# The second MoE's first layer as seven block products in two groups of 1024 tokens

## The chip, the cores and the metric

The kernel runs on one core of a Trainium2 chip. A core has TensorE (PE in the profile; its weight loads are PEld), VectorE (DVE), ScalarE (ACT), GpSimd (POOL) and the queue SyncE (SP), which here issues most DMAs; ScalarE's queue issues some. Each engine takes its instructions in order and waits at semaphores for the others. The metric is the device time of one execution in microseconds, the median of several runs.

## The reference

Three steps follow each other. An attention block reads 4 x 512 token rows against 32 state rows each and back, and gives N = 2176 rows (4 x (512 + 32)) of 512 numbers. A first MoE of 8 experts, whose gates are balanced over rows and columns, adds `P[:, e] * (relu(x @ w1[e]) @ w2[e])` over all experts. The second, the part changed here, is one dense layer pair:

```
h = x @ w_in                              # 2176 x 512 times 512 x 2048
g = h * (1.0 / (1.0 + np.exp(-h)))
return (g @ w_out).astype(np.float32)     # times 2048 x 512
```

`w_in` and `w_out` come as float64, everything else as float32.

## The kernel before

Every product of full precision is three matmuls of a high and a low half (fp32r): low x high, high x low, high x high (`mm3`, lines 84 to 86). A matmul has a stationary operand of 128 x 128 and streams up to 512 columns of the other.

The first MoE runs as 16 units (8 experts, two halves of 512 inner columns; line 618), each over 4 batches of 512 tokens and 4 blocks of 128 inner columns: `S1` makes the inner block with 6 matmuls, ScalarE takes its relu into `hh`, VectorE the low half `hl`, and two steps later (`LAG`) `S2` uses both in 12 matmuls of the second layer. The 128 state rows (tile 16) have their own small path (`sr_first`, `sr_turn`). Through units 2 to 15 `convert_some` slips the conversion of the float64 weights between the steps: 32 pieces of 128 x 512, each loaded by SP, nine VectorE operations and a ScalarE cast, then written to DRAM by one DMA from ScalarE's queue as high and low halves side by side (`convert`, line 230).

The second MoE has four slices `v` of 512 inner columns, run over five chunks of tokens (two of 512, three of 384, the state tile being one of them, line 553). Its `S1` streams the turned tokens `x2` (columns) past stationary blocks of `w_in`: 4 blocks of the model dimension x 3 = 12 matmuls for one inner block and chunk. ScalarE makes the sigmoid `sg`, VectorE the product `gv`, ScalarE the high half, VectorE the low half. `turn` (line 600) transposes the first MoE's result on PE, four tiles into one PSUM bank, in unit 15 and the first steps of the second MoE. `load_win` and `load_wout` fetch the converted weights a slice ahead.

PE's order is that of the code; a scheduler places the other engines' instructions. PSUM has eight banks: four for the second layer (`p2`), two for the first (`p1`), two for turns and small sums (`pm`).

## Time and profile before

| what | value |
| --- | --- |
| device time, median of 3 runs | 1671.8 us (1671.42 to 1672.97) |
| span of the profiled execution, first to last instruction (its own time outside the span is not recorded) | 1670.1 us |
| PE / VectorE / ScalarE busy | 1652.0 / 901.1 / 491.4 us |
| mean granted TensorE clock | 0.997 |
| DMA, mean | 133 GB/s |

Busy time counts an instruction from start to end; neighbouring matmuls overlap, so their starts, not their durations, tell what one costs. In the rows, `out<-in` names tiles without buffer numbers, `<-` after the idle time names what the engine waited for.

### The profile page before, as it was taken

The numbers are of one execution on the slowest core, as the hardware profiler recorded it, in microseconds if no ns is written. First come the engines' busy times: TensorE is split into PE (matmuls) and PEld (weight loads), VectorE is DVE, ScalarE is ACT, GpSimd is POOL, SyncE is SP. The second block draws the span as 40 slices with busy tenths as digits, with TensorE's granted clock in tenths as the row PEclk, the third lists the DMA queues.
The fourth block names the chain that finished last, engine by engine and source line by source line (L and its number), as shares of the span: only waits on it lengthen the run. The fifth ranks groups of instructions, "written<-read, shape, count | busy, mean of one in ns | idle before, by whom it ended". The sixth has DMA issues, their size and how long they took to land.

```text
span 1670.1 us, 19780 instructions
## 1 busy us (share of the span) xinstructions
PE 1652.0 (99%) x7660; PEld 1366.2 (82%) x7660; DVE 901.1 (54%) x1541; ACT 491.4 (29%) x887; POOL 15.6 (1%) x25
## 2 busy tenths in 40 slices
PE   7999999999999999999999999999999999999998
...
PEclk9999999999999999999999999999999999999999
...
GB/s 183 14 180 121 85 192 200 170 189 141 194 213 158 205 119 252 133 212 139 199 179 152 214 123 252 128 191 114 161 54 48 4 46 56 9 93 1 89 51 57
DMA packets 107628, 222.03 MB, mean 133 GB/s; under 512 B 28560, under 2 KB 44944, under 8 KB 107536
## 3 DMA queue, kind: packets, MB, share of 16 engines
q1 hardware_dynamic: 101152, 201.76, 41.2%
...
## 4 chain that ended last, share of the span: by engine, by line
PE 85%; DVE 0%; ACT 0%; issue 0%
PE po L84 17%; PE po L86 17%; PE po L85 17%; PE ph L84 10%; PE ph L86 10%; PE ph L85 10%; PE pg L463 3%; PE psr L85 1%; PE psr L86 1%; PE psr L84 1%; PE px L613 0%; PE pt L514 0%; DVE acc L585 0%; DVE l_w L89 0%; DVE accs L585 0%; ACT acc L588 0%
## 5 line engine op out<-in xcount | busy, mean ns | idle before, releaser
L84 PE MATMUL po<-h_w,hl 128*128 128x512 f32 x1024 | 403.1, 394 | 0.0
L86 PE MATMUL po<-h_w,hh 128*128 128x512 f32 x1024 | 398.9, 390 | 0.0
L85 PE MATMUL po<-l_w,hh 128*128 128x512 f32 x1024 | 398.8, 389 | 0.0
L535 DVE SCALAR_TENSOR_TENSOR hl<-ph,hh 128x512 fp32r<-128x512 f32 x256 | 176.6, 690 | 349.3 <-ACT hh L534 348.5
L534 ACT ACTIVATE hh<-ph 128x512 fp32r<-128x512 f32 x256 | 152.9, 597 | 593.6 <-PE ph L86 587.1
L84 PEld LDWEIGHTS po<-h_w,hl 128*128 128x128 f32 x1024 | 192.1, 188 | 50.2 <-issue 11.1
L86 PEld LDWEIGHTS po<-h_w,hh 128*128 128x128 f32 x1024 | 192.2, 188 | 40.6
L85 PEld LDWEIGHTS po<-l_w,hh 128*128 128x128 f32 x1024 | 192.3, 188 | 39.3 <-issue 0.2
L84 PE MATMUL ph<-aTh,G 128*128 128x512 f32 x512 | 203.6, 398 | 1.6 <-DVE hl L535 1.6
L86 PE MATMUL ph<-aTh,G 128*128 128x512 f32 x512 | 199.5, 390 | 0.0
L85 PE MATMUL ph<-aTl,G 128*128 128x512 f32 x512 | 199.5, 390 | 0.0
L589 DVE SCALAR_TENSOR_TENSOR acc<-po,P,acc 128x512 f32<-128x512 f32 x224 | 152.4, 741 | 4.1 <-PE po L86 4.1
L545 DVE TENSOR_TENSOR gv<-ph,sg 128x384 f32<-128x384 f32 (+1 forms) x80 | 48.8, 611 | 191.6 <-ACT sg L543 191.6
L89 DVE TENSOR_TENSOR l_w<-raw_w,h_w 128x512 fp32r<-128x512 f32 x128 | 87.6, 692 | 60.3 <-ACT h_w L203 58.9
L84 PE MATMUL ph<-x2h,wil 128*128 128x384 f32 (+1 forms) x320 | 115.6, 361 | 0.0
L86 PE MATMUL ph<-x2h,wih 128*128 128x384 f32 (+1 forms) x320 | 114.6, 358 | 0.0
L85 PE MATMUL ph<-x2l,wih 128*128 128x384 f32 (+1 forms) x320 | 114.4, 358 | 0.0
L84 PEld LDWEIGHTS ph<-aTh,G 128*128 128x128 f32 x512 | 96.2, 188 | 21.3 <-DVE hl L535 1.9
L86 PEld LDWEIGHTS ph<-aTh,G 128*128 128x128 f32 x512 | 96.1, 188 | 20.4
L85 PEld LDWEIGHTS ph<-aTl,G 128*128 128x128 f32 x512 | 96.2, 188 | 19.2 <-DVE aTl L89 0.2
L543 ACT ACTIVATE sg<-ph 128x384 f32<-128x384 f32 (+1 forms) x80 | 42.7, 534 | 220.5 <-PE ph L86 217.9
L86 PE MATMUL po<-woh,hh 128*128 128x512 f32 x272 | 106.8, 393 | 0.0
...
## 6 DMA issues: line engine op xcount, KB each, us to landing
g_d<-stg SPq DMA_DIRECT2D x120, 512.0 KB, 3.9
G<-g_d SPq DMA_DIRECT2D x240, 256.0 KB, 5.7
raw_w<-in_moe_w_dram SPq DMA_DIRECT2D x136, 256.0 KB, 5.6
raw<-in_moe_w_in_dram SPq DMA_DIRECT2D x16, 512.0 KB, 6.4
wi_d<-cvo ACTq DMA_DIRECT2D x16, 512.0 KB, 2.6
raw<-in_moe_w_out_dram SPq DMA_DIRECT2D x16, 512.0 KB, 6.4
wo_d<-cvo ACTq DMA_DIRECT2D x16, 512.0 KB, 3.2
x<-in_x_dram SPq DMA_DIRECT2D x16, 256.0 KB, 4.1
```

The source lines that it names most:

```text
L84: nc.tensor.matmul(ps, al, bh, start=first, stop=False)
L85: nc.tensor.matmul(ps, ah, bl, start=False, stop=False)
L86: nc.tensor.matmul(ps, ah, bh, start=False, stop=last)
L89: engine.tensor_tensor(out=lo, in0=src, in1=hi.bitcast(F32), op=ALU.subtract)
L463: nc.tensor.matmul(pg[hp, half], a[lanes[half], hp], w[lanes[half]], start=i == 0, stop=i == 2)
L534: nc.scalar.activation(out=hh, in_=ph, func=AF.Relu)
L535: last["dve"] = nc.vector.scalar_tensor_tensor(out=hl, in0=ph, scalar=0.0, in1=hh.bitcast(F32), op0=ALU.max, op1=ALU.subtract)
L543: nc.scalar.activation(out=sg[:, :n], in_=ph[:, :n], func=AF.Sigmoid)
L545: nc.vector.tensor_tensor(out=gv[:, :n], in0=ph[:, :n], in1=sg[:, :n], op=ALU.mult)
L589: nc.vector.scalar_tensor_tensor(out=a, in0=ps, scalar=P[:, t, e:e + 1], in1=a, op0=ALU.mult, op1=ALU.add)
```

## The change

The first layer of the second MoE is computed for two groups of 1024 tokens (eight tiles each). For a slice of 256 inner columns (`phases`: 2 groups x 4 slices `v` x 2 halves `fp` = 16) it is a product of 2 x 2 blocks: two blocks of 128 inner columns, two halves of the model dimension (256 each), two chunks of 512 tokens. Instead of eight block products it takes seven, in Winograd's form of Strassen's scheme: products 1, 2 and 4 take blocks of the weights as they are, the other four sums of them; of the tokens, 1, 2 and 3 take blocks, the others sums. A product is 2 x 3 = 6 matmuls of 512 columns (`product`). Products 1, 6, 7, 4 are added one after another in one PSUM bank, 5 and 3 in another, 2 in a third; ScalarE copies what must be kept between them (`s1`, `s5`, `u2`, `u3`), VectorE adds the parts (`c11`, `c12`, `c22`).

The four sums of weight blocks are made once, in the first MoE, by `convert_in`, which handles two row blocks of `w_in` at a time; its results go to DRAM in pieces of 128 partitions x 2 x 128 (`wi_d`) and as whole rows (`wr_d`). The sums of token blocks are made by `tokens` from float32 copies of the turned tokens (`turn`), for group 0 in unit 15 and for group 1 in phases 6 and 7. Each phase loads the next phase's seven weights behind its own products. Between the products the second layer of the phase before runs in four parts (`second`); the results have tiles of their own (`res`).

The state tile no longer shares a chunk: its turned tokens are stationary and the rows of `w_in` stream past them in 12 matmuls of 512 columns for each `v` (`s_first`, in two halves), its result is turned back (`s_back`) and goes through the second layer in `s_second`.

```diff
+    def convert_in(v, kp):
+
+        both = att.tile([128, 2, FU], F32, tag="att", name=f"wb_{v}_{kp}")
+        for j in range(2):
+            k = kp + 2 * j
+            src = w_in[k * 128:(k + 1) * 128, 2 * v * FU:2 * (v + 1) * FU]
+            tf, af = yield from halves_of(src, f"i{v}_{k}")
+            w = both[:, j]
+            yield V.tensor_tensor(out=w, in0=tf, in1=af, op=ALU.add)
+            hl = att.tile([128, 2, FU], F32R, tag="att", name=f"cvi_{v}_{k}")
+            nc.scalar.copy(hl[:, 0], w)
+            yield V.tensor_tensor(out=hl[:, 1], in0=w, in1=hl[:, 0].bitcast(F32), op=ALU.subtract)
+            nc.scalar.dma_start(out=wr_d[v][k], in_=hl.bitcast(F32))
+            tiles = hl.bitcast(F32).rearrange("p s (f i c) -> p s f i c", f=2, i=2)
+            for i in range(2):
+                if (i, j) != (1, 0):
+                    for s in range(2):
+                        nc.scalar.dma_start(out=wi_d[v][i + j, :, :, s, kp, :].rearrange("f p c -> p f c"), in_=tiles[:, s, :, i])
+        sums = att.tile([128, 4, 2, 128], F32, tag="att", name=f"ws_{v}_{kp}")
+        w4 = both.rearrange("p j (f i c) -> p j i f c", f=2, i=2)
+        a11, a12, a21, a22 = w4[:, 0, 0], w4[:, 1, 0], w4[:, 0, 1], w4[:, 1, 1]
+        yield V.tensor_tensor(out=sums[:, 0], in0=a21, in1=a22, op=ALU.add)
+        yield V.tensor_tensor(out=sums[:, 1], in0=sums[:, 0], in1=a11, op=ALU.subtract)
+        yield V.tensor_tensor(out=sums[:, 2], in0=a11, in1=a21, op=ALU.subtract)
+        yield V.tensor_tensor(out=sums[:, 3], in0=a12, in1=sums[:, 1], op=ALU.subtract)
+        hi, lo = (att.tile([128, 4, 2, 128], F32R, tag="att", name=f"ws{i}_{v}_{kp}") for i in "hl")
+        m = "p m f c -> p (m f c)"
+        nc.scalar.copy(hi.rearrange(m), sums.rearrange(m))
+        yield V.tensor_tensor(out=lo.rearrange(m), in0=sums.rearrange(m), in1=hi.bitcast(F32).rearrange(m), op=ALU.subtract)
+        for s, t in enumerate((hi, lo)):
+            for i in range(4):
+                nc.scalar.dma_start(out=wi_d[v][3 + i, :, :, s, kp, :].rearrange("f p c -> p f c"), in_=t.bitcast(F32)[:, i])
+
...
+    def load_win(v, fp, p):
+        tag = "w1h" if loaded[0] % 2 == 0 else "w1l"
+        loaded[0] += 1
+        w = wp.tile([128, 2, 2, 128], F32R, tag=tag, name=f"wi_{v}_{fp}_{p}_{loaded[0]}", bufs=4)
+        nc.sync.dma_start(out=w.bitcast(F32), in_=wi_d[v][WEIGHT_OF[p], fp])
+        went[p] = w
+
...
         hT[u, b, f] = (hh, hl)
 
...
+    def turn(g, c, k):
+
+        j, kp = divmod(k, 2)
+        if kp == 0:
+            F2[g, j, c] = stp.tile([128, 2, 512], F32, tag="stg", name=f"x2f_{g}_{j}_{c}")
+        pt = pm(f"px2_{g}_{c}_{k}")
+        for i, t in enumerate(chunks[2 * g + c]):
+            nc.tensor.transpose(pt[:, i * 128:(i + 1) * 128], acc_of(t)[:, k * 128:(k + 1) * 128], ident)
+        nc.scalar.copy(F2[g, j, c][:, kp], pt)
+
+    def tokens(g, p, pool=s8, tag="s8"):
+
+        flat = "p k c -> p (k c)"
+        made = {5: ((0, 1), (0, 0)), 6: ((1, 1), 5), 7: ((1, 1), (0, 1)), 4: ((1, 0), 6)}
+        if p in made:
+            src = F2[g, p] = att.tile([128, 2, 512], F32, tag="att", name=f"x2t_{g}_{p}")
+            one, other = (F2[(g, *at) if isinstance(at, tuple) else (g, at)] for at in made[p])
+            nc.vector.tensor_tensor(out=src.rearrange(flat), in0=one.rearrange(flat), in1=other.rearrange(flat), op=ALU.subtract)
...
+            src = F2[g, *{1: (0, 0), 2: (1, 0), 3: (1, 1)}[p]]
+        x = x2[g, p] = pool.tile([128, 2, 2, 512], F32R, tag=tag, name=f"x2_{g}_{p}")
+        nc.scalar.copy(x[:, 0].rearrange(flat), src.rearrange(flat))
+        lo_of(x[:, 1].rearrange(flat), src.rearrange(flat), x[:, 0].rearrange(flat))
+
+    def product(q, p):
+
+        g, v, fp = phases[q]
+        where = {1: "a", 6: "a", 7: "a", 4: "a", 2: "b", 5: "c", 3: "c"}[p]
+        if p in (1, 2, 5):
+            banks[where] = p1(f"pa{q}") if where == "a" else pm(f"p{where}{q}")
+        ps, w, x = banks[where], went[p], x2[g, p]
+        for kp in range(2):
+            ops = ((w[:, 1, kp], x[:, 0, kp]), (w[:, 0, kp], x[:, 1, kp]), (w[:, 0, kp], x[:, 0, kp]))
+            for i, (a, b) in enumerate(ops):
+                begin = p in (1, 2, 5) and kp == 0 and i == 0
+                nc.tensor.matmul(ps, a, b, start=begin, stop=kp == 1 and i == 2, skip_group_check=True)
+
+        if p == 1:
+            kept("s1", "e2", att)
+        elif p == 5:
+            kept("s5", "att", att)
+        elif p == 2:
+            silu(q, 0, 0, summed("c11", ps, parts["s1"]))
+        elif p == 6:
+            kept("u2", "e2", att)
+        elif p == 3:
+            silu(q, 0, 1, summed("c12", ps, parts["u2"]))
+        elif p == 7:
+            kept("u3", "att", att)
+            silu(q, 1, 1, summed("c22", parts["u3"], parts["s5"]))
+        else:
+            silu(q, 1, 0, ps)
+
+    def silu(q, f, c, src):
+        sg = att.tile([128, 512], F32, tag="e2", name=f"sg{q}_{f}_{c}", bufs=3)
+        nc.scalar.activation(out=sg, in_=src, func=AF.Sigmoid)
+        nc.vector.tensor_tensor(out=sg, in0=src, in1=sg, op=ALU.mult)
+        hh = hp_.tile([128, 512], F32R, tag="hh", name=f"gh{q}_{f}_{c}")
+        hl = hp_.tile([128, 512], F32R, tag="hl", name=f"gl{q}_{f}_{c}")
+        nc.scalar.copy(hh, sg)
+        lo_of(hl, sg, hh)
+        blocks[q, f, c] = hh, hl
+
...
+        if f == 0:
+            res_p[q, c] = [bank(f"pr{q}_{t}") for t in tiles]
+        hh, hl = blocks.pop((q, f, c))
+        wh, wl = w2t[g, v, 2 * fp + f]
+        for i, ps in enumerate(res_p[q, c]):
+            s = slice(i * 128, (i + 1) * 128)
+            mm3(ps, hh[:, s], hl[:, s], wh, wl, f == 0, f == 1)
...
+    def s_load(v, half):
+        t = wr[v, half] = s8.tile([128, 2, 2, FU], F32R, tag="s8", name=f"wr_{v}_{half}")
+        nc.sync.dma_start(out=t.bitcast(F32), in_=wr_d[v][2 * half:2 * half + 2].rearrange("k p s f -> p k s f"))
+
+    def s_first(v, half):
+        if half == 0:
+            sp[v] = pm(f"psf{v}")
+        w = wr.pop((v, half))
+        for i in range(2):
+            k = 2 * half + i
+            mm3(sp[v], sx["h"][:, k], sx["l"][:, k], w[:, i, 0], w[:, i, 1], k == 0, k == KD - 1)
+        if half == 1:
+            ps = sp.pop(v)
+            t = sg_of[v] = att.tile([128, FU], F32, tag="e2", name=f"sgs{v}", bufs=3)
+            nc.scalar.activation(out=t, in_=ps, func=AF.Sigmoid)
+            nc.vector.tensor_tensor(out=t, in0=ps, in1=t, op=ALU.mult)
...
-    convert_ops = (op for i in range(NV * (KD + NF)) for op in convert(i))
-    pace = 10 * NV * (KD + NF) / ((NU - 2.5) * B * NF)
+    convert_ops = convert_all()
+    pace = 1.12 * NV * (2 * 23 + NF * 9) / ((NU - 2.5) * B * NF)
     done = [0]
...
+            if u == NU - 1 and 8 <= k < 12:
+                for n in range(2):
+                    turn(0, k % 2, (k - 8) // 2 * 2 + n)
+            if u == NU - 1 and k == 12:
+                s_load(0, 0)
+            if u == NU - 1 and k in (8, 9, 10, 11, 12, 13):
+                for p in {8: (1,), 9: (5,), 10: (2,), 11: (6, 3), 12: (7,), 13: (4,)}[k]:
+                    tokens(0, p)
+
+    ending = [lambda: S2(*steps[-2]), lambda: None, lambda: S2(*steps[-1]), lambda: None]
+    for q, (g, v, fp) in enumerate(phases):
+        more = q + 1 < len(phases)
+        earlier = ending if q == 0 else [lambda n=n: second(q - 1, n) for n in range(4)]
+
+        def step(p):
+            product(q, p)
+            if more:
+                load_win(*phases[q + 1][1:], p)
+            if q == 7 and p != 4:
+                later = {1: 6, 5: 3, 2: 7, 6: 4}.get(p)
+                if later:
+                    tokens(1, later)
+
+        s0 = g == 0 and fp == 0
+        step(1)
+        step(5)
+        step(2)
+        earlier[0]()
+        if q == 0:
+            load_wout(0, 0, 2)
+            s_turn()
+        elif g == 0 and fp == 1:
+            s_back(v)
+        step(6)
+        earlier[1]()
+        if s0:
+            s_first(v, 0)
+            s_load(v, 1)
+        step(3)
+        step(7)
+        earlier[2]()
+        if s0:
+            s_first(v, 1)
             if v + 1 < NV:
-                if b == 3 and f < 2:
-                    load_win(v + 1, f)
-                if b == 4:
-                    if f < 2:
-                        load_win(v + 1, f + 2)
-                    load_wout(v + 1, f)
+                s_load(v + 1, 0)
+        if 3 <= q < 7:
+            turn(1, (q + 1) % 2, (q - 3) // 2 * 2)
+            turn(1, (q + 1) % 2, (q - 3) // 2 * 2 + 1)
+        step(4)
+        earlier[3]()
+        if q == 0:
+            load_wout(0, 0, 3)
+        if g == 0 and fp == 1:
+            s_second(v, 0)
+        elif q and q <= 8 and fp == 0:
+            s_second(phases[q - 1][1], 1)
+        if more:
+            for f in range(2):
+                g1, v1, fp1 = phases[q + 1]
+                if q:
+                    load_wout(g1, v1, 2 * fp1 + f)
+        if q == 6:
+            for p, (pool, tag) in zip((1, 5, 2), ((s8, "s8"), (accp, "acc"), (accp, "acc"))):
+                tokens(1, p, pool, tag)
+    q = len(phases) - 1
+    spare = iter((p1, p1, pm, pm))
+    for n in range(4):
+        second(q, n, p2 if n < 2 else lambda nm: next(spare)(nm))
```

Three places show how the instructions stand. First ScalarE's queue in the first MoE's unit 2, around the conversion: before, one cast `cvo` and one DMA for each piece (`L260`, `wi_d0`), between relus `hh` and weight casts `h_w`; the brackets name the semaphores waited for, `DMAHW` those of earlier DMAs.

```order
L257 CAST cvo_1_2524<-cv_1_2365 128x512 [waits DVE_49]
L534 ACTIVATE hh2_2_1_2534<-ph2_2_1_2527 128x512 [waits PE_49,Activation_49]
L203 CAST h_w1_4_0_2576<-raw_w1_4_0_2574 128x512 [waits DMAHW4_49]
L260 DMA wi_d0_174<-cvo_1_2524 128x1024 [waits DMAHW0_49,DVE_49,Activation_49]
L534 ACTIVATE hh2_2_2_2587<-ph2_2_2_2580 128x512 [waits PE_49]
L203 CAST h_w1_4_1_2615<-raw_w1_4_1_2613 128x512 [waits DMAHW6_49]
L534 ACTIVATE hh2_2_3_2631<-ph2_2_3_2624 128x512 [waits PE_49]
L517 CAST hsh_3_2652<-pt_3_2647 128x512 [waits PE_49]
L534 ACTIVATE hh2_3_0_2675<-ph2_3_0_2668 128x512 [waits PE_49]
```

And now, same place, where the sums of the first pair of row blocks (`wsh`, `wsl`) are written:

```order
L287 CAST wsh_0_0_2624<-ws_0_0_2540 128x1024 [waits DVE_49]
L291 DMA wi_d0_178<-wsh_0_0_2624 128x2x128 [waits Activation_49]
L291 DMA wi_d0_178<-wsh_0_0_2624 128x2x128 [waits DMAHW1_49]
L291 DMA wi_d0_178<-wsh_0_0_2624 128x2x128 [waits DMAHW2_49]
L577 ACTIVATE hh2_2_3_2646<-ph2_2_3_2639 128x512 [waits PE_49]
L291 DMA wi_d0_178<-wsh_0_0_2624 128x2x128 [waits DMAHW3_49]
L291 DMA wi_d0_178<-wsl_0_0_2625 128x2x128 [waits DMAHW5_49,DVE_49]
L291 DMA wi_d0_178<-wsl_0_0_2625 128x2x128 [waits DMAHW6_49]
L291 DMA wi_d0_178<-wsl_0_0_2625 128x2x128 [waits DMAHW7_49]
L291 DMA wi_d0_178<-wsl_0_0_2625 128x2x128 [waits DMAHW0_49]
L561 CAST hsh_3_2667<-pt_3_2662 128x512 [waits PE_49]
L577 ACTIVATE hh2_3_0_2702<-ph2_3_0_2695 128x512 [waits PE_49]
```

One DMA has become eight in a row (others of three and five stand ahead), seven of which wait for the semaphore of an earlier DMA; the relu `hh2_3_0` and the turned state rows `hsh` stand behind them.

Second PE where a group of four tiles is turned (`px2`). Before, early in the second MoE:

```order
L85 MATMUL po16_0_3_10714<-wol_0_1_10577,hh16_0_1_10654 128x512
L86 MATMUL po16_0_3_10714<-woh_0_1_10575,hh16_0_1_10654 128x512
L613 MATMUL px2_3_1_10768<-ident_98,acc2_1250 128x128 [waits DVE_49]
L613 MATMUL px2_3_1_10768<-ident_98,acc3_1450 128x128 x2
L84 MATMUL ph16_1_0_10774<-x2h_1_10471,wil_0_0_10162 128x512 [waits DVE_49]
L85 MATMUL ph16_1_0_10774<-x2l_1_10472,wih_0_0_10160 128x512
L86 MATMUL ph16_1_0_10774<-x2h_1_10471,wih_0_0_10160 128x512
L84 MATMUL ph16_1_0_10774<-x2h_1_10471,wil_0_0_10162 128x512
L85 MATMUL ph16_1_0_10774<-x2l_1_10472,wih_0_0_10160 128x512
```

Now, in phase 6, after the second half of the state tile's first layer (`psf3`, weights `wr_3_1`):

```order
L84 MATMUL psf3_12065<-wr_3_1_12072,sxl_10865 128x512 [waits DMAHW0_49]
L85 MATMUL psf3_12065<-wr_3_1_12072,sxh_10864 128x512
L86 MATMUL psf3_12065<-wr_3_1_12072,sxh_10864 128x512
L84 MATMUL psf3_12065<-wr_3_1_12072,sxl_10865 128x512
L85 MATMUL psf3_12065<-wr_3_1_12072,sxh_10864 128x512
L86 MATMUL psf3_12065<-wr_3_1_12072,sxh_10864 128x512
L629 MATMUL px2_1_1_2_12136<-ident_98,acc2_1254 128x128 [waits DVE_49]
L629 MATMUL px2_1_1_2_12136<-ident_98,acc2_1254 128x128
L629 MATMUL px2_1_1_2_12136<-ident_98,acc3_1454 128x128 x2
L629 MATMUL px2_1_1_3_12142<-ident_98,acc2_1254 128x128 [waits Activation_49]
L629 MATMUL px2_1_1_3_12142<-ident_98,acc2_1254 128x128
L629 MATMUL px2_1_1_3_12142<-ident_98,acc3_1454 128x128 x2
```

Two groups are turned one behind the other, the second waits for ScalarE's copy of the first, and the phase's product 4 and a part of the second layer come behind both; the state's second half waits for its own load.

Third VectorE. Before, at the start of slice 2:

```order
L545 TENSOR_TENSOR gv17_4_3_12030<-ph17_4_3_12015,sg17_4_3_12028 128x384 [waits Activation_49]
L89 TENSOR_TENSOR hl17_4_3_12033<-gv17_4_3_12030,hh17_4_3_12032 128x384 [waits Activation_49]
L545 TENSOR_TENSOR gv18_0_0_12068<-ph18_0_0_12053,sg18_0_0_12066 128x512 [waits Activation_49]
L89 TENSOR_TENSOR hl18_0_0_12071<-gv18_0_0_12068,hh18_0_0_12070 128x512 [waits PE_49,Activation_49]
L545 TENSOR_TENSOR gv18_0_1_12102<-ph18_0_1_12087,sg18_0_1_12100 128x512 [waits Activation_49]
L585 TENSOR_TENSOR accs_1468<-po17_4_16_11995,accs_1468 128x512 [waits PE_49]
L585 TENSOR_TENSOR acc3_1450<-po17_4_14_11996,acc3_1450 128x512 [waits PE_49]
```

Now, where phase 7 begins (`ress` is the state tile's result, `c11_7` the phase's first sum, `gls3` the state's low half):

```order
L775 TENSOR_TENSOR ress_11152<-prs2_1_12179,ress_11152 128x512 [waits PE_49]
L89 TENSOR_TENSOR x2_1_5_12200<-x2t_1_5_12198,x2_1_5_12200 128x1024
L89 TENSOR_TENSOR x2_1_2_12203<-x2f_1_1_0_11923,x2_1_2_12203 128x1024
L89 TENSOR_TENSOR x2_1_6_12219<-x2t_1_6_12217,x2_1_6_12219 128x1024 [waits PE_49,Activation_49]
L89 TENSOR_TENSOR x2_1_3_12233<-x2f_1_1_1_12135,x2_1_3_12233 128x1024 [waits PE_49,Activation_49]
L667 TENSOR_TENSOR c11_7_12243<-pb7_12236,s1_7_12213 128x512 [waits PE_49]
L639 TENSOR_TENSOR x2t_1_7_12254<-x2f_1_1_1_12135,x2f_1_0_1_11720 128x1024
L689 TENSOR_TENSOR sg7_0_0_12245<-c11_7_12243,sg7_0_0_12245 128x512 [waits Activation_49]
L89 TENSOR_TENSOR gls3_12281<-pst3_12275,ghs3_12280 128x512 [waits Activation_49]
L89 TENSOR_TENSOR x2_1_7_12256<-x2t_1_7_12254,x2_1_7_12256 128x1024 [waits Activation_49]
L89 TENSOR_TENSOR gl7_0_0_12249<-sg7_0_0_12245,gh7_0_0_12248 128x512 [waits Activation_49]
```

Operations of 1024 columns for group 1's tokens (`x2_1_...`) stand in the row ahead of the phase's own work.

## Rows read from the trace of the kernel before

**Rows 1.** The page: span, busy time, PE and granted clock in 40 slices.

```profile
span 1670.1 us, 19780 instructions
## 1 busy us (share of the span) xinstructions
PE 1652.0 (99%) x7660; PEld 1366.2 (82%) x7660; DVE 901.1 (54%) x1541; ACT 491.4 (29%) x887; POOL 15.6 (1%) x25
...
PE   7999999999999999999999999999999999999998
...
PEclk9999999999999999999999999999999999999999
```

**Rows 2.** The page, chain of waits: shares by engine.

```profile
PE 85%; DVE 0%; ACT 0%; issue 0%
```

**Rows 3.** Stretches: their us, busy time of each engine, clock, DMA share, GB/s.

```profile
700.00:1100.00 400.00, 400.00 (x1811) 327.19 (x1810) 241.66 (x392) 111.74 (x195) 0.00 (x0) 1.00 0.60 183
...
1400.00:1500.00 100.00, 100.00 (x473) 86.75 (x472) 36.43 (x60) 23.04 (x42) 0.00 (x0) 1.00 0.13 43
```

**Rows 4.** PE's timeline, end of the second MoE: start us, duration, instruction.

```profile
1657.11 0.33 PE L84 MATMUL ph<-x2h,wil 128*128 128x384 f32 x1
...
1659.22 0.39 PE L84 MATMUL po<-woh,hl 128*128 128x512 f32 x1
...
1661.07 0.39 PE L86 MATMUL po<-woh,hh 128*128 128x512 f32 x1
...
1665.15 0.39 PE L86 MATMUL po<-woh,hh 128*128 128x512 f32 x1
```

**Rows 5.** PE's timeline around a turned group in unit 15.

```profile
1245.22 0.60 PE L613 MATMUL px<-ident,acc 128*128 128x128 f32 x4
1245.57 0.49 PE L84 MATMUL ph<-aTh,G 128*128 128x512 f32 x1
...
1249.80 0.39 PE L84 MATMUL po<-h_w,hsl 128*128 128x512 f32 x1
```

**Rows 6.** The page, costliest groups: busy us, mean ns of one, idle before.

```profile
L535 DVE SCALAR_TENSOR_TENSOR hl<-ph,hh 128x512 fp32r<-128x512 f32 x256 | 176.6, 690 | 349.3 <-ACT hh L534 348.5
L534 ACT ACTIVATE hh<-ph 128x512 fp32r<-128x512 f32 x256 | 152.9, 597 | 593.6 <-PE ph L86 587.1
...
L89 DVE TENSOR_TENSOR l_w<-raw_w,h_w 128x512 fp32r<-128x512 f32 x128 | 87.6, 692 | 60.3 <-ACT h_w L203 58.9
```

**Rows 7.** ScalarE's timeline: the copy of that group.

```profile
1245.86 0.59 ACT L614 CAST x2h<-px 128x512 fp32r<-128x512 f32 x1 [2.56 <-PE px L613]
```

**Rows 8.** Lines 152 and 89 by shape: duration ns min/median/max, first and last start.

```profile
L152 ACT CAST bdh<-bd x1: 1047/1047/1047, 11.9 to 11.9; 128x1024 fp32r<-128x1024 f32 x1
...
L89 DVE TENSOR_TENSOR bdl<-bd,bdh x1: 1226/1226/1226, 13.0 to 13.0; 128x1024 fp32r<-128x1024 f32 x1
```

**Rows 9.** DMA: queues (packets, MB, share of 16 engines); issues, median us to landing.

```profile
q1 hardware_dynamic: 101152, 201.76, 41.2%
...
wi_d<-cvo ACTq DMA_DIRECT2D x16, 512.0 KB, 2.6
...
wih<-wi_d SPq DMA_DIRECT2D x16, 256.0 KB, 3.2
```

**Rows 10.** Line 260 on ScalarE's queue: ns of its waits and issues.

```profile
L260 ACTq EVENT_SEMAPHORE  x32: 17/1932/4564, 243.3 to 1130.9; - x32
L260 ACTq DMA_DIRECT2D wi_d<-cvo x16: 326/326/337, 247.1 to 1017.1; - x16
```

**Rows 11.** Waits in 300 to 1240: us in total, times, longest.

```profile
ACT hh L534 <- PE ph L86: 503.1, 197, 6.2
```

More of the change, by code (lines that the diff above doesn't have):

```diff
@@ new lines, in convert_all @@
+    def convert_all():
+        for v in range(NV):
+            for kp in range(2):
+                yield from convert_in(v, kp)
+            for f in range(NF):
+                yield from convert_out(v, f)
+    PRODUCTS = (1, 5, 2, 6, 3, 7, 4)
+    WEIGHT_OF = {1: 0, 2: 1, 3: 6, 4: 2, 5: 3, 6: 4, 7: 5}
+    went = {}
+    loaded = [0]
+    def load_win(v, fp, p):
[4 more added lines that the diff above has]
+        went[p] = w
@@ new lines, in S1 @@
+        gh, gl = G[u, b][:, :, 0], G[u, b][:, :, 1]
+        ah, al = (t[:, b % 2] for t in aT[b // 2])
+        fs = slice(f * 128, (f + 1) * 128)
+        for q in range(2):
+            mm3(ph, gh[:, q, fs], gl[:, q, fs], ah[:, q], al[:, q], q == 0, q == 1)
+        hh = hp_.tile([128, 512], F32R, tag="hh", name=f"hh{u}_{b}_{f}")
+        hl = hp_.tile([128, 512], F32R, tag="hl", name=f"hl{u}_{b}_{f}")
+        nc.scalar.activation(out=hh, in_=ph, func=AF.Relu)
+        last["dve"] = nc.vector.scalar_tensor_tensor(out=hl, in0=ph, scalar=0.0, in1=hh.bitcast(F32), op0=ALU.max, op1=ALU.subtract)
@@ L618, in fused_kernel @@
-    steps = [(u, b, f) for u in range(NU + NV) for b in range(B if u < NU else len(chunks)) for f in range(NF)]
+    F2, x2 = {}, {}
+    def turn(g, c, k):
[6 more added lines that the diff above has]
+        nc.scalar.copy(F2[g, j, c][:, kp], pt)
@@ new lines, in fused_kernel, with kept, summed @@
+    banks, parts, blocks = {}, {}, {}
+    def product(q, p):
[4 more added lines that the diff above has]
+        ps, w, x = banks[where], went[p], x2[g, p]
+        for kp in range(2):
+            ops = ((w[:, 1, kp], x[:, 0, kp]), (w[:, 0, kp], x[:, 1, kp]), (w[:, 0, kp], x[:, 0, kp]))
+            for i, (a, b) in enumerate(ops):
+                begin = p in (1, 2, 5) and kp == 0 and i == 0
+                nc.tensor.matmul(ps, a, b, start=begin, stop=kp == 1 and i == 2, skip_group_check=True)
+        def kept(nm, tag, pool):
+            t = parts[nm] = pool.tile([128, 512], F32, tag=tag, name=f"{nm}_{q}", **({"bufs": 3} if tag == "e2" else {}))
+            nc.scalar.copy(t, ps)
+        def summed(nm, one, other):
+            t = rawp.tile([128, 512], F32, tag="raw", name=f"{nm}_{q}")
+            nc.vector.tensor_tensor(out=t, in0=one, in1=other, op=ALU.add)
+            return t
+        if p == 1:
[13 more added lines that the diff above has]
+            silu(q, 1, 0, ps)
@@ new lines, in second @@
+    def second(q, n, bank=p2):
+        g, v, fp = phases[q]
+        c, f = divmod(n, 2)
+        first, final = (v, fp) == (0, 0), (v, fp) == (NV - 1, 1)
+        tiles = chunks[2 * g + c]
+        if f == 0:
[5 more added lines that the diff above has]
+            mm3(ps, hh[:, s], hl[:, s], wh, wl, f == 0, f == 1)
+        if f == 0:
+            return
+        if first:
+            res[g, c] = accp.tile([128, 4, DM], F32, tag="acc", name=f"res{g}_{c}")
+        for i, (t, ps) in enumerate(zip(tiles, res_p.pop((q, c)))):
+            a = res[g, c][:, i]
+            if first:
+                nc.vector.tensor_copy(a, ps)
+            else:
+                nc.vector.tensor_tensor(out=a, in0=ps, in1=a, op=ALU.add)
+            if final:
+                b, r = divmod(t, R)
+                (nc.sync if t % 2 else nc.scalar).dma_start(out=out[b * ROWS:b * ROWS + S].rearrange("(p r) d -> p r d", r=R)[:, r], in_=a)
```

151 lines of the change are left out of this document (58 added, 93 removed).

## Prediction

> **What bounds the kernel now.** I read the page first. TensorE (PE) is busy 99% of the span and its granted clock stands at 9 tenths or more in every slice, the upper of its two levels, 2.4 GHz; VectorE is busy 54%, ScalarE 29% [rows 1]. The chain of waits puts 85% of the span on PE and next to nothing on any other engine [rows 2]. The table by stretches says the same for the two places the change touches: in the first MoE (700 to 1100) PE has no gap, VectorE is busy 60%, ScalarE 28%, and the DMA engines 0.60; in the second (1400 to 1500) PE again has none, VectorE is at 36%, ScalarE at 23%, DMA at 0.13 [rows 3]. So the end is the sum of PE's instructions, and the price of one is the step from a matmul's start to the next one's, not the duration in its row (0.39), which overlaps with its neighbours. Eighteen second-layer matmuls of 512 columns start from 1661.07 to 1665.15: 4.08/18 = 0.2267 us each. Twelve first-layer matmuls of 384 columns take from 1657.11 to 1659.22: 2.11/12 = 0.1758 each [rows 4].
>
> The sum is made against the profiled execution, whose span is 1670.1; the median of the runs is 1671.8, so 1.7 lie around the span or between executions, and I carry them over unchanged.
>
> **First layer, on PE.** Before, each of 16 column blocks takes 12 matmuls for each of five token chunks: 384 of 512 columns and 576 of 384 columns, 384 x 0.2267 + 576 x 0.1758 = 87.1 + 101.3 = 188.3 us. Now: 16 phases x 7 products x 6 matmuls = 672, and 4 x 12 = 48 for the state tile, all of 512 columns: 720 x 0.2267 = 163.2. Difference -25.1. The second layer stays at 816 matmuls of 512 columns. The products have another order and another pair of operands, but the same shape, so I take the same step for them.
>
> The Trainium skill speaks against the full size of this term: "TensorE: Matmul & The Clock Gate", section "Back-to-back issue gap", puts the isolated warm step at N/2.4 + 2.5 ns, thus 216 and 162.5 ns, by which the estimate would be 720 x 0.2158 - 384 x 0.2158 - 576 x 0.1625 = -21.1. The trace does not agree: the steps are 227 and 176 ns [rows 4], and the sum goes by these.
>
> **Transposes.** 84 in 21 groups of four instead of 68 in 20 groups. One group of four: from 1245.22 to 1249.80 lie the group and 18 matmuls; 4.58 - 18 x 0.2267 = 0.50 us [rows 5]. Sixteen more transposes are +2.0 (between +0.5 for one more group and +2.0).
>
> **What waits in the steady phases.** One phase is 90 matmuls, 20.4 us of PE. ScalarE has 12 operations (4 copies, 4 sigmoids, 4 casts) at 0.60, VectorE 19 (3 sums, 4 products with the sigmoid, 4 low halves, 8 result adds) at 0.69 [rows 6]: 7.2 us (35%) and 13.1 us (64%). Products 1, 6, 7, 4 go one after another into one bank, so each waits until ScalarE has copied what stood there. Closest is product 4 behind the copy u3: between product 7 and it lies one part of the second layer, 12 x 0.2267 = 2.72 us. The sum c12 and one sigmoid stand before the copy on ScalarE, and end about 0.3 after product 7; the copy takes 0.60: about 0.9 to 1.1 of 2.72. The other hand-offs have 0.5 to 1.8 us left. I take 0; if the cover is gone it costs what rival C says.
>
> **The turn into group 1.** In phases 4 and 6 the state tile's sums hold one of the two banks for transposes, so the second group of four waits for ScalarE's copy of the first. In the trace the transposes start at 1245.22, and their copy begins at 1245.86 and takes 0.59 [rows 5, 7]: ready at 1246.45, where the second group would have started at 1245.72. That is 0.75, and 1.0 with part of the state's sigmoid ahead on ScalarE: 2 x 1.0 = +2.0 (0 to 4). Phases 6 and 7 also carry the casts of group 1: VectorE has 42 operations at 0.69 and 11 of 1024 wide at 1.23 [rows 6, 8], 42.5 us, where PE has 204 matmuls and 3 groups of transposes, 47.7 us. At 89% in order, behind four low halves of 1.23 in a row, something comes late: the state's transposed tile waits behind c11_7, the state's second-layer bank behind the result adds. By hand four such places give 0.4 + 0.9 + 0.5 + 0.8 = +2.6 (0 to 6). The turn into the first phase, during unit 15, has seven casts of 1.05 on ScalarE and as many low halves on VectorE [rows 8]; everything is ready but the state tile's low half: +0.2 (0 to 2).
>
> **The state weights' second half.** It may be loaded only when the first half has been read, and is wanted three steps later: 1.36 + 1.36 + 2.72 = 5.44 us. A 256 KB piece lands in 3.2 us. SP's queue moved 201.76 MB in 41.2% of the span: 293 GB/s. So 1 MB costs 3.2 - 0.89 + 3.58 = 5.9 [rows 9]; 0.45 x 4 = +1.8. Bounds: 0, and +12 if it shares the engines with the seven weights (3.0 each). All other loads are issued nearly a phase ahead of their use.
>
> **The conversion, in the first MoE.** VectorE gets 40 more operations, about 21 us over some 900 where it is 60% busy [rows 3]: hidden. ScalarE gets 8 casts of 1024 (1.05 [rows 8]) and issues 144 DMAs in place of 32, in 8 bursts each of three, five and eight. Issuing one takes 0.326, and ahead of each of the 32 the queue stood 1.93 us in the median (0.02 to 4.56) at a semaphore [rows 10]; part of that is VectorE's low half, part the DMA that used the same semaphore before, here often one of SP's. All of this stands ahead of the relus, which the next units need. Before each relu ScalarE now idles 503.1/197 = 2.6 us [rows 11]; a relu may come 5.3 us late (two banks: the next use of a bank is 30 matmuls, 6.8 us, after it was filled, less 0.60 + 0.69 and hand-offs). The short bursts fit (five: 1.6 + 1.9). A burst of eight: 2.6 of issue, 1.9 of wait, and one landing of 2.6 [rows 9] are 7.1; but the scheduler puts relus between its DMAs. I take 0.5 for each of eight bursts: +4 (0 to 36, below).
>
> The Trainium skill, "DMA: Bandwidth & Descriptors", section "Issuing engines are not separate DMA queues", calls the time to initiate a DMA usually small beside the DMA itself. Here it is 0.33 beside 2.6 [rows 9, 10], which agrees; by that rule alone this term would be 0 and the sum -16.5, but the rule counts no waits ahead of the issue, and the row has them.
>
> **Sum.** -25.1 + 2.0 + 2.0 + 2.6 + 0.2 + 1.8 + 4 = -12.5: a span of 1657.6, and 1659.3 for the median. The tail (last add, last output) is the same kind of work. Own range by half and double the waits: 1653 to 1668.
>
> **Rivals.**
> B, all added waits are hidden: -25.1 + 2.0 = -23.1, 1648.7. For it: no engine but PE is above 64% in a steady phase, and before, the PE row shows no waiting at all [rows 3]. Against it: only one bank is free for the turns, which no faster engine mends.
> C, a hand-off in every phase: product 4 waits for u3, or the second layer for a low half. If each of 16 phases loses 0.8, that is +12.8 on top of the sum: 1672.1, no change. For it: seven products have four strict hand-offs where before two banks took turns. Against it: the row order on ScalarE puts u3 ahead of the cast that waits for VectorE, which leaves the slack above.
> D, slower: the first MoE pays, because ScalarE stands at the semaphores of its own 512-byte-piece DMAs and of SP's loads, and relus and copies of the gate products behind it come late. Without the +4 the sum is -16.5; it turns when 24 bursts lose over 0.69 us each. At 1.5 each, 36 us: 1671.8 - 16.5 + 36 = 1691. For it: the wait of 1.93 before a single DMA [rows 10], and that SP's G loads in turn wait for ScalarE's DMAs. Against it: 2.6 us of idle time before each relu [rows 11], and 32 such waits that left PE without a gap.
> E, the change doesn't do what it says: products with a slower step than 0.2267 (other reading pattern, or the clock lower in the gaps). At the 384-column price per column (0.1758/384 x 512 = 0.2344) the 672 cost 5.2 more: 1664.5. It stays on the forecast's side.
>
> **How the numbers follow.** Forecast 0.45 (with E), B 0.23, C 0.17, D 0.12, unnamed 0.03. The predicted time is the forecast's, 1659. A measurement of this kernel tells 0.2%, 3.3 us, from no change. Faster: 0.45 + 0.23 + 0.10 of C + 0.02 = 0.80; same: 0.06 of C and a little of D, 0.08; slower 0.12. The range leaves out the far side of B and D: 1646 to 1675.
>
> **What would show it.** The second MoE, from its first first-layer matmul to PE's last one, 15 to 20 us shorter, with PE gaps of about 1 us at the second turns of phases 4 and 6, at the state's second halves, and at the start of phases 7 and 8, and none in phases 9 to 15. In the first MoE, intervals between units longer by 0 to 1 us. If units grow by 2 us or more, D is right and the forecast wrong; if PE waits before product 4 in every phase, C; if the product step is not 0.2267, the first term falls.

## Result and profile after

The changed kernel takes 1648.5 us in the median (1647.6 to 1649.1) beside 1672.3 for the kernel before in the same rounds: a ratio of 0.9857, 95% interval 0.9843 to 0.987. That is 23.8 us faster; forecast were 12.5, and the number lies within the stated range, 1646 to 1675, nearly on rival B (all added waits hidden, 1648.7).

The page of the changed kernel, first its span, busy times, clock row, DMA queues and the shares of the chain, which answer to [rows 1, 2, 9]:

```profile
span 1645.7 us, 19928 instructions
## 1 busy us (share of the span) xinstructions
PE 1627.0 (99%) x7436; PEld 1328.8 (81%) x7436; DVE 1004.9 (61%) x1676; ACT 543.2 (33%) x946; POOL 15.6 (1%) x25
...
PEclk9999999999999999999999999999999999999999
...
q1 hardware_dynamic: 107168, 239.52, 48.5%
q10 hardware_dynamic: 36848, 33.71, 6.2%
...
PE 94%; DVE 3%; ACT 1%; DMA 1%; issue 1%; SPq 0%; DVEq 0%; ACTq 0%
```

The same stretches as [rows 3] (us, then busy PE, PEld, DVE, ACT, POOL, clock, DMA share, GB/s):

```profile
1400.00:1500.00 100.00, 99.21 (x448) 81.65 (x448) 69.54 (x100) 40.01 (x64) 0.00 (x0) 1.00 0.47 154
...
700.00:1100.00 400.00, 399.33 (x1807) 326.35 (x1807) 249.02 (x411) 115.05 (x200) 0.00 (x0) 1.00 0.65 198
```

PE is as full as before, though VectorE has nearly doubled (36 to 70) in the second MoE, and ScalarE's queue (`q10`) has six times the packets. PE's waits in the changed kernel (us in total, times, longest), the two largest behind the kernel's start:

```profile
PE px L629 <- ACT x2f L630: 1.6, 2, 0.8
PE po L84 <- DVE acc L617: 1.3, 3, 0.7
```

The first row is the forecast wait of the second turned group, 0.8 in place of 1.0 at each of two places. None stands before a product, a part of the second MoE's second layer, or the state's transposes. The second row lies in the first MoE, three places that the kernel before does not have; it is taken up under the conversion below.

Where the time went can be read with one marker: `hs`, the state rows' relu, runs once in each unit, its last in unit 15, ahead of the turns. First before, then after (first and last start):

```profile
L507 ACT ACTIVATE hs<-psr x16: 598/599/600, 138.8 to 1176.9; 128x512 f32<-128x512 f32 x16
```

```profile
L551 ACT ACTIVATE hs<-psr x16: 588/598/600, 136.7 to 1175.7; 128x512 f32<-128x512 f32 x16
```

From the first to the last `hs` the first MoE took 1038.1 us before and 1039.0 after, so the conversion costs 0.9 in this pair of profiles; nine profiles of kernels with this same first MoE go from 1039.0 to 1040.6. From the last `hs` to the span's end it was 1670.1 - 1176.9 = 493.2, and now 1645.7 - 1175.7 = 470.0: the second MoE gained 23.2. The 2.1 before the first `hs` lie at the start, which the change doesn't touch; the first `hs` stands at 136.7 to 138.9 in the profiles of this kernel and of the runs below. This split is used for all of them ("second part" below; the changed kernel has 470.0 and, run again, 469.9).

### The profile page after: what moved, and what is told of

Read it like the earlier page. It is cut to its first block, busy times and chain, and to the rows that moved or that the text cites. A ratio compares the mean times of both kernels' runs of the same rounds, so it can differ in the third digit from the quotient of the medians.

```text
span 1645.7 us, 19928 instructions
## 1 busy us (share of the span) xinstructions
PE 1627.0 (99%) x7436; PEld 1328.8 (81%) x7436; DVE 1004.9 (61%) x1676; ACT 543.2 (33%) x946; POOL 15.6 (1%) x25
## 4 chain that ended last, share of the span: by engine, by line
PE 94%; DVE 3%; ACT 1%; DMA 1%; issue 1%; SPq 0%; DVEq 0%; ACTq 0%
PE po L84 15%; PE po L86 14%; PE po L85 14%; PE ph L84 7%; PE ph L86 7%; PE ph L85 7%; PE pa L659 5%; PE pr L85 4%; PE pr L86 4%; PE pr L84 4%; PE pg L507 3%; PE pc L659 3%; PE pb L659 1%; PE psr L418 1%; PE psr L84 1%; PE psr L86 1%
## 5 line engine op out<-in xcount | busy, mean ns | idle before, releaser
L84 PEld LDWEIGHTS ph<-aTh,G 128*128 128x128 f32 x512 | 96.2, 188 | 21.6 <-DVE hl L578 2.1
L203 ACT CAST h_w<-raw_w 128x512 fp32r<-128x512 f32 x136 | 81.8, 621 | 94.1 <-PE po L86 46.4
L84 PE MATMUL pr<-woh,gl 128*128 128x512 f32 x256 | 99.6, 389 | 0.0
L86 PE MATMUL pr<-woh,gh 128*128 128x512 f32 x256 | 99.6, 389 | 0.0
L85 PE MATMUL pr<-wol,gh 128*128 128x512 f32 x256 | 99.6, 389 | 0.0
L659 PE MATMUL pa<-x,wi 128*128 128x512 f32 x384 | 98.3, 392 | 0.0
L89 DVE TENSOR_TENSOR stg<-pg,stg 128x512 fp32r<-128x512 f32 x120 | 75.7, 684 | 27.1 <-ACT stg L512 27.0
```

The source lines that it names most:

```text
L84: nc.tensor.matmul(ps, al, bh, start=first, stop=False)
L85: nc.tensor.matmul(ps, ah, bl, start=False, stop=False)
L86: nc.tensor.matmul(ps, ah, bh, start=False, stop=last)
L89: engine.tensor_tensor(out=lo, in0=src, in1=hi.bitcast(F32), op=ALU.subtract)
L203: nc.scalar.copy(hi, raw)
L659: nc.tensor.matmul(ps, a, b, start=begin, stop=kp == 1 and i == 2, skip_group_check=True)
```

## Experiments

**Eight products in place of seven.** No sums of weights or tokens; every block of C gets its two products in a bank of its own.

```diff
-        where = {1: "a", 6: "a", 7: "a", 4: "a", 2: "b", 5: "c", 3: "c"}[p]
...
+        f, c, j = p
+        if j == 0:
+            banks[f, c] = (p1 if f == c else pm)(f"p{f}{c}_{q}")
+        ps, w, x = banks[f, c], went[2 * f + j], x2[g, 2 * j + c]
...
-        step(3)
-        step(7)
+        step((1, 1, 1))
+        step((1, 0, 0))
```

> The changed kernel with its groups, phases, state path and order, but each phase multiplies the 2 x 2 blocks out in eight block products in place of seven, without sums of weights or tokens. Theory A (the end is the sum of PE's steps, everything else is hidden): 16 phases x 6 matmuls x 0.2267 = 21.8 us more than the changed kernel, a span of about 1667.5 and a median near 1670, 2 us below the kernel before. Theory B (the products' copies and hand-offs cost something that the trace of waits does not show): less than 21.8 more, since these are gone too; 5 us less would be about 1665.

Measured: 1675.3 us, ratio to before 1.0019 (1.0009 to 1.0028): 26.8 more than the changed kernel, more than either theory said. Of B's sign, less than 21.8, nothing is seen, but waits that came new could hide it. The trace names most of the rest: PE waits before turned groups, which here find both banks for turns taken.

```profile
PE px L614 <- DVE sgs L706: 2.9, 2, 1.5
PE px L614 <- ACT x2f L615: 2.9, 4, 0.8
```

**Eight products, the turned groups where banks are free.**

```diff
-        if 3 <= q < 7:
-            turn(1, (q + 1) % 2, (q - 3) // 2 * 2)
-            turn(1, (q + 1) % 2, (q - 3) // 2 * 2 + 1)
         step((1, 0, 1))
+        if 3 <= q < 7:
+            turn(1, (q + 1) % 2, (q - 3) // 2 * 2)
         earlier[3]()
+        if 3 <= q < 7:
+            turn(1, (q + 1) % 2, (q - 3) // 2 * 2 + 1)
```

> Eight block products as before (kernel eight, 26.8 us above the changed kernel, with 5.8 us of waits of PE before turned groups where the changed kernel has 1.6), but the turned groups of phases 3 to 6 stand behind product 8 and behind the second layer's last part, where banks are free. Theory A: without those waits only the 16 x 6 x 0.2267 = 21.8 us of the eighth product are left, and the 1.6 of the changed kernel's own two waits go too: 20 to 22 above the changed kernel, 1668.5 to 1670.5. If 26 remain, the eighth product costs more than its matmuls.

Measured: 1667.3 us, 0.9972 (0.9959 to 0.9984), 18.8 above the changed kernel, 1.2 below the range expected, and 19.7 to 20.4 above the changed kernel with its own turns apart (next). No wait of PE is listed in the second part any more. It is 1666.0 - 1175.5 = 490.5, against 1644.9 - 1176.2 = 468.7 there: 21.8, theory A's number. The `hs` rows, of this kernel and of the next one (its second profile):

```profile
L536 ACT ACTIVATE hs<-psr x16: 598/598/600, 137.8 to 1175.5; 128x512 f32<-128x512 f32 x16
```

```profile
L551 ACT ACTIVATE hs<-psr x16: 591/598/600, 136.8 to 1176.2; 128x512 f32<-128x512 f32 x16
```

The first MoE gives the difference, 1037.7 without the sums against 1039.0 to 1040.6. So in the second MoE leaving out the eighth product is worth its matmuls, no more and no less, and the sums of weights take 1 to 3 us of that back in the first.

**The turned groups on both sides of product 4**, twice, the second time beside the changed kernel itself.

```diff
             turn(1, (q + 1) % 2, (q - 3) // 2 * 2)
-            turn(1, (q + 1) % 2, (q - 3) // 2 * 2 + 1)
         step(4)
+        if 3 <= q < 7:
+            turn(1, (q + 1) % 2, (q - 3) // 2 * 2 + 1)
```

> The changed kernel, but in phases 3 to 6 the second group of four transposes comes behind product 4 instead of behind the first group. The two waits of 0.8 for ScalarE's copy in the trace of after should go, 1.6 us less than the changed kernel: a span of about 1644 and a median near 1647. If the wait is only moved (product 4 then holds something that the turned group waits for), no change.

> The changed kernel itself, on the same chip and beside the same runs as the next kernel: 1648.5 again, the measure for it.

> The changed kernel with the two turned groups of phases 3 to 6 on both sides of product 4, as before. If the two waits of 0.8 us are really gained, 1.6 less than the changed kernel beside it; if the 1.6 of the first comparison was chance, within 0.5 of it.

Measured: 1646.95 (0.9853, 0.9838 to 0.9868) and 1647.6 (0.9849, 0.9836 to 0.9862); the changed kernel again 1648.6 (0.9859, 0.9846 to 0.9873). The intervals overlap, so the medians alone don't settle it. The trace does: the wait of PE before turned groups has gone, and the second part is 468.7 in both profiles against 470.0 and 469.9. A gain of 1.2 us, not quite the 1.6 that were expected (a wait of 0.2 before a `pr` bank is new); its medians are the lowest of all the kernels here.

**The copy u3 made three and five times over.**

```diff
-            kept("u3", "att", att)
+            u3 = parts["u3"] = att.tile([128, 512], F32, tag="att", name=f"u3_{q}")
+            for _ in range(5):
+                nc.scalar.copy(u3, ps)
```

> The changed kernel, but ScalarE makes the copy u3 five times over, so product 4 is released 2.4 us later in each phase (the cast ahead of the last copies adds up to 0.6). By the slack that the prediction gave (0.9 to 1.1 of 2.72 us used) PE waits 0.8 to 1.4 in each of 16 phases: 13 to 22 us more than the changed kernel, 1662 to 1670, rival C made real. If the cover is larger than read, no change (1648.5).

> The changed kernel, but the copy u3 made three times over: product 4 is released 1.2 us later in each phase. With five copies (2.4 us and up to one cast more) the loss was 16.9 us, 1.06 in each phase, so 1.3 to 1.9 of the cover is free: three copies stay inside it, no change (within 2 us of the changed kernel). If ScalarE's row as a whole is what costs, half of the 16.9: 8 us more.

Measured: five copies 1665.4 (0.9961, 0.9946 to 0.9976), 16.9 more; three 1649.95 (0.9868, 0.9853 to 0.9882), 1.4 more. With five, PE waits where rival C said:

```profile
PE pa L659 <- ACT u L683: 7.6, 10, 0.8
PE px L629 <- ACT x2f L630: 3.6, 2, 2.2
```

The listed 7.6 is less than the loss: the second part is 15.2 longer, 1.0 a phase in the mean. With three no wait before product 4 is listed; the second part is 1.5 longer, 0.6 of it before turned groups (2.2 in place of 1.6). 1.2 us are covered, 2.4 are not: some 1.4 are free, near the 1.6 to 1.8 that the prediction read from the order of ScalarE's queue, and C needs more than that to come true.

**The weight pieces in twice as many DMAs.**

```diff
-                        nc.scalar.dma_start(out=wi_d[v][i + j, :, :, s, kp, :].rearrange("f p c -> p f c"), in_=tiles[:, s, :, i])
+                        for h in range(2):
+                            nc.scalar.dma_start(out=wi_d[v][i + j, h, :, s, kp, :], in_=tiles[:, s, h, i])
...
-                nc.scalar.dma_start(out=wi_d[v][3 + i, :, :, s, kp, :].rearrange("f p c -> p f c"), in_=t.bitcast(F32)[:, i])
+                for h in range(2):
+                    nc.scalar.dma_start(out=wi_d[v][3 + i, h, :, s, kp, :], in_=t.bitcast(F32)[:, i, h])
```

> The changed kernel, but every 128 KB piece of the converted weights goes out as two DMAs of 64 KB: 224 in place of 112 on ScalarE's queue, bursts of 16 in place of 8. Slack theory: ScalarE pays 112 x 0.48 = 54 us more of issue, but PE sees only what passes 5.3 us in front of a relu: a burst of 16 takes 7.7 of issue, so 0 to 2.4 in each of 8: 0 to 19 us more, most likely under 5. Rival D as it was meant (ScalarE's queue is near its limit): 20 to 50 us more.

Measured: 1653.2 (0.9892, 0.9877 to 0.9907), 4.7 more. The first MoE takes 1043.6 in place of 1039.0; the second part is unchanged (469.8). The loss has one kind of place, where the gate products `pg` need a bank that a late `hl` still holds:

```profile
PE pg L509 <- DVE hl L580: 4.7, 4, 1.4
```

One of the four, 0.4, is in the changed kernel too; the other three, 1.43 to 1.44 each, are new. They do not stand behind bursts of 16, after which no wait of PE is listed, but behind bursts of nine, which are five in the changed kernel. ScalarE's, VectorE's and PE's rows at the first of them: six DMAs, the last of the nine, end where the relu `hh` starts.

```profile
560.94 3.19 ACTq L278 DMA_DIRECT2D wi_d<-cvi  x6
564.17 0.60 ACT L579 ACTIVATE hh<-ph 128x512 fp32r<-128x512 f32 x1 [4.75 <-DMA wi_d<-cvi]
565.55 0.50 PE L509 MATMUL pg<-h_w,stl 64*128 64x512 f32 x1 [1.43 <-DVE hl L580]
```

So rival D's mechanism exists. The number expected, under 5, came true, but at another place than the one it was worked out for.

**VectorE's low halves of group 1's operands made twice.**

```diff
-        lo_of(x[:, 1].rearrange(flat), src.rearrange(flat), x[:, 0].rearrange(flat))
+        for _ in range(1 + g):
+            lo_of(x[:, 1].rearrange(flat), src.rearrange(flat), x[:, 0].rearrange(flat))
```

> The changed kernel, but VectorE makes the low half of each of group 1's seven token operands twice: 7 x 1.23 = 8.6 us more of VectorE in phases 6 and 7. By the prediction's count (42.5 of 47.7 us of VectorE, 2.6 us of waits already) VectorE would now be the longer of the two, 51.1 of 47.7: 3.4 + 2.6 or more, 6 to 9 us more than the changed kernel. By the trace of after, which has no wait of PE there, part of the 5.2 us of room is still free and the operations that PE wants go ahead of the others: 0 to 4 us more.

Measured: 1657.0 (0.9908, 0.9894 to 0.9923), 8.5 more. PE stops at the place that the prediction named, the state's transposes behind `c11_7`, and goes on at the lower clock: product 6 takes 2.7 us from its start to the next matmul's, where it takes 1.36 at the upper level. VectorE's `c` and PE's timeline, then the clock by stretches (third number from the right):

```profile
1455.58 0.68 DVE L668 TENSOR_TENSOR c<-pb,s 128x512 f32<-128x512 f32 x1
1456.32 1.12 PE L760 MATMUL pst<-ident,sgs 128*128 128x128 f32 x4 [5.34 <-DVE c L668]
1457.08 2.91 PE L660 MATMUL pa<-x,wi 128*128 128x512 f32 x6
1459.79 0.63 PE L84 MATMUL pr<-woh,gl 128*128 128x512 f32 x1
```

```profile
1450.00:1456.00 6.00, 0.97 (x5) 0.47 (x3) 6.00 (x6) 0.00 (x0) 0.00 (x0) 0.89 0.10 35
1456.00:1459.00 3.00, 2.69 (x9) 2.30 (x10) 3.00 (x4) 2.15 (x4) 0.00 (x0) 0.50 0.00 0
```

The number is on the prediction's side, but by luck: its count had VectorE longer than PE (51.1 of 47.7 us), while by the steps read below VectorE has 37.3 + 7 x 1.14 = 45.3. What is lost is one stop of 5.34, and some 2.4 at the lower clock behind it: 7.7 of the 7.9 by which the second part is longer.

**The state weights' second half: load queued later, and use moved closer.**

```diff
             s_first(v, 0)
-            s_load(v, 1)
         step(3)
+        if s0:
+            s_load(v, 1)
```

> The changed kernel, but the load of the state weights' second half is issued one product later, so that 4.08 us of PE's work lie in front of its use instead of 5.44. By the landing that the trace of after shows (4.9 us in the median) PE waits about 0.8 at each of four places: 3 us more than the changed kernel, and a wait of PE on this load appears in the trace. By the prediction's estimate of 5.9 us it would be 1.8 each, 7 us more. If the load's end is not what releases PE, no change.

Measured: 1649.4 (0.9861, 0.9844 to 0.9877), no change, and the trace shows why it tells nothing: SP does not wait for the product, only for the slot, so the load is issued at the same point, 1.55 us after the first half's first matmul, in both kernels (1427.71 to 1429.26 in the changed kernel, 1430.65 to 1432.21 here). The second kernel moves the use instead:

```diff
         step(7)
-        earlier[2]()
         if s0:
             s_first(v, 1)
             if v + 1 < NV:
                 s_load(v + 1, 0)
+        earlier[2]()
```

> The changed kernel, but the state tile's second half is computed ahead of the second layer's part that stood between: 2.72 us of PE's work after the first half in place of 5.44, with the load of 1 MB issued at the same point. By the 4.9 us of the trace of after (from issue to landing; the issue comes 0.2 after the first half's last matmul has started) PE waits 2.2 to 2.6 at each of four places: 9 to 10 us more than the changed kernel, a little more if the clock falls in the gaps. By the prediction's 5.9: 3.2 to 3.5 each, 13 to 14 us more.

Measured: 1658.9 (0.9926, 0.9912 to 0.9939), 10.4 more, the first of the two numbers. The wait is there four times, one of them in PE's timeline:

```profile
1342.99 0.50 PE L84 MATMUL psf<-wr,sxl 128*128 128x512 f32 x1 [2.16 <-DMA wr<-wr_d]
```

## Why the prediction was half right

**First layer, -25.1: right.** The product's step is the 0.2267 of [rows 4], a product's six matmuls taking 1.36, so rival E is out:

```profile
1278.85 1.52 PE L659 MATMUL pa<-x,wi 128*128 128x512 f32 x6
1280.21 1.52 PE L659 MATMUL pc<-x,wi 128*128 128x512 f32 x6
```

Of the 25.1, 21.8 are the eighth product, as the experiment shows. The other 3.3 come from the new groups and the state tile's path (816 x 0.2267 = 185.0 with eight products, 188.3 before); the kernel with eight products and free banks has a second part 2.7 shorter than before's, where these 3.3 less one or so for the transposes would make some 2. The Trainium skill's isolated step ("TensorE: Matmul & The Clock Gate", section "Back-to-back issue gap"), which gave -21.1, would by the sum below have left the second part 4 us longer than the rows' step does: the measurement decides for the rows.

**Transposes, +2.0: too much.** Turned in pairs, eight cost 0.90 (the pairs of unit 15 start at 1254.88 and 1259.86, with 18 matmuls between: 4.98 - 4.08, rows below), less than two groups of 0.50 [rows 5]. With 0.50 each for the other five groups that is 9.7 now; before, eight groups of 0.50 and twelve of three transposes at 0.39 (for one: 1298.22 to 1304.05 less 24 matmuls, 5.83 - 5.44) made 8.7. So +1.0.

```profile
1254.88 1.03 PE L629 MATMUL px<-ident,acc 128*128 128x128 f32 x8
1259.86 1.03 PE L629 MATMUL px<-ident,acc 128*128 128x128 f32 x8
```

**Turned groups, +2.0: right in kind, 1.2 to 1.6 in size.**

**VectorE in phases 6 and 7, +2.6: this step failed, and it is the most instructive.** The sum took 0.69 and 1.23, the durations of [rows 6, 8], as the price of an operation. But neighbouring operations of VectorE overlap too. VectorE's timeline of the changed kernel at the start of phase 7:

```profile
1444.06 0.68 DVE L775 TENSOR_TENSOR ress<-prs,ress 128x512 f32<-128x512 f32 x1
1444.65 1.22 DVE L89 TENSOR_TENSOR x<-x2t,x 128x1024 fp32r<-128x1024 f32 x1
1445.79 1.22 DVE L89 TENSOR_TENSOR x<-x2f,x 128x1024 fp32r<-128x1024 f32 x1
1446.92 1.22 DVE L89 TENSOR_TENSOR x<-x2t,x 128x1024 fp32r<-128x1024 f32 x1
1448.06 1.22 DVE L89 TENSOR_TENSOR x<-x2f,x 128x1024 fp32r<-128x1024 f32 x1
1449.19 0.69 DVE L667 TENSOR_TENSOR c<-pb,s 128x512 f32<-128x512 f32 x1
```

Back to back, the step from start to start is 0.59 and 1.14. 42 x 0.59 + 11 x 1.14 = 37.3 us of 47.7, not 42.5. `c` ends at 1449.88, and the transposes that wait for it start on time:

```profile
1450.13 0.60 PE L759 MATMUL pst<-ident,sgs 128*128 128x128 f32 x4
```

That is 0.25 us behind the end of `c`; the hand-off itself took 0.06 where PE did wait (1456.32 against 1455.58 + 0.68), so 0.2 are to spare, where the prediction had a wait, one of its four of 0.4 to 0.9. By durations, 1444.06 + 0.68 + 4 x 1.22 + 0.69, `c` would have ended at 1450.31, too late. The place was the right one, as the doubled low halves show, and there is next to no room in it: five more operations ahead of `c` (5 x 1.14 = 5.7 us) gave a wait of 5.34.

**State weights, +1.8: the term was mis-sized.** 1 MB lands in 4.9 us, not 5.9:

```profile
wr<-wr_d SPq DMA_DIRECT2D x8, 1024.0 KB, 4.9
```

Issued as the first half's last matmul ends, it is in time by 0.3 for PE's matmul in the last of the four (1429.26 + 4.9 against 1434.51). In the first of the four it is not quite: PE's weight load waits for it, which costs PE 0.1 (the next matmul starts 0.33 later in place of 0.23). SP's row and that of the weight load:

```profile
1289.35 0.37 SPq L740 DMA_DIRECT2D wr<-wr_d  x1
1294.59 0.19 PEld L84 LDWEIGHTS psf<-wr,sxl 128*128 128x128 f32 x1 [0.26 <-DMA wr<-wr_d]
```

The estimate had used the queue's mean rate over its busy share, 293 GB/s; from 256 KB in 3.0 to 1 MB in 4.9 the added 0.79 MB go at about 410, an estimate from the two landings.

**The turn into the first phase, +0.2: right in place, 0.1 in size.** PE's weight load waits 0.44 for the state tile's low half (`sxl`), and again the matmul behind it steps by 0.33.

**Conversion, +4: 0.9 measured in this pair of profiles, up to 2.5 in the others.** Here is the first burst of eight on ScalarE's queue, with the relus around it:

```profile
281.96 1.05 ACT L287 CAST wsh<-ws 128x1024 fp32r<-128x1024 f32 x1 [1.09 <-DVE ws L284]
283.04 1.42 ACTq L291 DMA_DIRECT2D wi_d<-wsh  x3
284.51 0.60 ACT L577 ACTIVATE hh<-ph 128x512 fp32r<-128x512 f32 x1 [1.50 <-PE ph L86]
284.53 0.47 ACTq L291 DMA_DIRECT2D wi_d<-wsh  x1
285.10 2.13 ACTq L291 DMA_DIRECT2D wi_d<-wsl  x4
287.51 0.59 ACT L561 CAST hsh<-pt 128x512 fp32r<-128x512 f32 x1 [2.41 <-PE pt L558]
288.90 0.60 ACT L577 ACTIVATE hh<-ph 128x512 fp32r<-128x512 f32 x1 [0.80 <-PE ph L86]
```

A DMA stands 0.48 us in the median, more than the 0.33 of [rows 10] (0.37 to 1.71; how much of that is a wait inside it, the rows don't part). But no wait of length stands ahead of it; where line 291 on ScalarE's queue has rows of waits, they show (ns, min/median/max):

```profile
L291 ACTq EVENT_SEMAPHORE  x15: 17/17/17, 285.0 to 1026.8; - x15
```

So the 1.93 of [rows 10] was no price of an earlier DMA. It was VectorE's low half, for which line 260 also waits: in the kernel before, each of the 32 DMAs starts 0.07 to 0.09 us after that low half's end. The first of them:

```profile
246.32 0.68 DVE L259 TENSOR_TENSOR cvo<-cv 128x512 fp32r<-128x512 f32 x1
247.08 0.34 ACTq L260 DMA_DIRECT2D wi_d<-cvo  x1
```

Both relus around the burst of eight still wait for PE and not the other way round. What PE does lose stands elsewhere: the three waits for VectorE's adds, 1.3 us, which neither the kernel before nor the two with eight products have. The largest, 0.67, is rival D's mechanism in the changed kernel itself. A burst of five DMAs (720.64 to 724.79) keeps ScalarE from a weight cast, VectorE waits for the cast, and its adds free a bank late:

```profile
724.83 0.62 ACT L203 CAST h_w<-raw_w 128x512 fp32r<-128x512 f32 x1 [4.23 <-DMA wi_d<-cvi]
725.49 0.69 DVE L89 TENSOR_TENSOR l_w<-raw_w,h_w 128x512 fp32r<-128x512 f32 x1 [4.15 <-ACT h_w L203]
728.50 0.50 PE L84 MATMUL po<-h_w,hsl 128*128 128x512 f32 x1 [0.67 <-DVE acc L617]
```

The prediction had put the cost at bursts of eight and called those of five short enough; a burst's cost hangs on what stands behind it, and not on its length alone. The Trainium skill's rule on issue costs ("DMA: Bandwidth & Descriptors", section "Issuing engines are not separate DMA queues": small beside the DMA itself, 0.48 beside 2.7 to 5.0 here) came nearer than the term that I took from the row.

**The sum again:** -25.1 + 1.0 + 1.2 to 1.6 + 0.9 = -21.6 to -22.0 of the profiles' 24.4, the 0.1 at each of two weight loads left aside; 2.1 lie ahead of the first unit, which the change doesn't touch, and 0.3 behind PE's last matmul. That the time fell on B's 1648.7 is partly luck: 2 to 3 us of waits did come, and the start and the cheaper transposes make up for them. The forecast's own range, 1653 to 1668, missed (and double its 12.6 of added terms would be 1672, not 1668); the stated one held because it takes in B. The sign it named, a second MoE 15 to 20 us shorter from its first first-layer matmul to PE's last, reads 22.6: 1280.33 to 1665.15 before, 1278.85 to 1641.07 after. The forecast's error was one-sided: the waits were priced by upper numbers (a duration, a mean rate, a median of waits of another kind), and a wait that is not reached costs nothing at all, so B deserved more than its 0.23.
